# Layers two and four of an attention and two-MLP kernel, with Strassen's steps as the outer loop

## The chip, the cores and the metric

The kernel runs on one core of a Trainium2 chip. The metric is the device time of one execution in microseconds (us). TensorE (PE) does the matrix products, VectorE (DVE), ScalarE (ACT) and GpSimd (POOL) prepare operands and take results out of PSUM, and the queues of SP, ACT and POOL issue the DMAs.

## The reference

Causal attention over 2 x 12 heads (448 positions, head width 64) gives x of 896 x 768. Two MLPs follow, each with an inner width of 2048:

```python
x = attn_out.transpose(0, 2, 1, 3).reshape(896, 768)
h = x @ moe_w_in                                        # layer 1
g = np.maximum(h, 0) + alpha * np.minimum(h, 0)
x = g @ moe_w_out                                       # layer 2
h = x @ moe2_w_in                                       # layer 3
g = np.where(h >= 1, h, np.where(h <= -1, 0, (h + 1) ** 2 / 4))
out = g @ moe2_w_out                                    # layer 4
```

## The kernel before

Every operand of a product is held as a high and a low part, each in a 4-byte format that TensorE multiplies; a product of two 128-deep tiles takes three matmuls of 448 columns (high x high, high x low, low x high). A tile of the left side is `[128, 2, 448]`, for one depth tile and one batch `b` (0 or 1). Weights come from HBM as 8-byte numbers into `w_raw`, SP issues the DMA. The helper `cast` makes the upper piece `top` of each number (line L226, on POOL), `join` puts a 4-byte weight together from `w_raw` and `top` on DVE (L235), ACT makes the high part of `w_split` (L272 for layers 1 and 3, L547 for layers 2 and 4) and DVE subtracts to get the low part (L276, L552). `w_split` has three buffers.

Layers 1 and 3 (`run_layer`, products at L443) loop over 16 tiles `f` of the inner width, 36 matmuls each. `activate` (L360 to L370) and `split_g` (L347, L348) make the left tiles of the next layer from the results, and `sum_ops` (L397 to L409) makes sums S1 to S4 of them.

Layers 2 and 4 (`class Strassen`, products at L647) treat the product as a 2 x 2 block product. Its blocks are the two batches, the left and right half of the 768 output columns, and two parts of the depth. `NPAIR = 6` pairs of depth tiles, 12 of the 16, go through Strassen's scheme: seven products in place of eight, with weight quarters B11, B12, B21, B22, their sums T1 to T4 (`weight_sum`, L527, L530, L533, L536), and left sides A11, A12, A22 and S1 to S4. The last four depth tiles (`FREE`) are multiplied plainly, as items `n0` and `n2`. The loop outside is `m`, the three groups of 128 output columns in each half; inside it run the nine `ITEMS`. So every left side is gone through once for each `m`.

S2, S3 and S4 are written to DRAM by `keep`, and read back by `load_left` (L619) into places that are named by hand (`place`, the tags `g..`), then split again by ACT (`left_high`, L623) and DVE (`left_low`, L627). As there are not places for all, three tiles of each of A12, A22 and S4 (`SHIFTED`) are read again from DRAM for every further `m` (`AGAIN`, `RELOAD`; names beginning with `sA` in the trace). `copies` (L685, ACT) takes partial results out of PSUM, and `total` (L691 in layer 2, L699 in layer 4) adds the rest. In layer 2 the results of `m` 0 and 1 also go to DRAM and come back (`load_kept`, L589).

The program is written in the order in which each engine executes it: no scheduler moves anything. Each engine works through its own queue in order, and a wait at its head holds up all behind it.

Of the kernel before, what the change touches and what calls it, by code (L numbers as in the profile page):

```python
# [8 lines left out]
F32 = mybir.dt.float32  # L9
# [13 lines left out]
def attention_moe_moe_kernel(ctx: ExitStack, tc: tile.TileContext, qk, v, w1, w2, w3, w4, alpha, out):  # L23
# [8 lines left out]
    nc = tc.nc  # L32
# [86 lines left out]
    class Weights:  # L119


        def __init__(self):
            self.chunks, self.full, self.home = [], [], []
            for layer in (1, 3):
                w_in = {1: w1, 3: w3}[layer]
                for f in ORDER[layer][2 * (layer > 1):]:
                    self.add_full(w_in[f])
                self.add(layer, 0, "n0")
                for m in range(MH):
                    for i in range(len(ITEMS)):  # L130
# [973 lines left out]
```

## Time and profile before

| | us |
|---|---|
| median of 3 runs | 531.25 (529.7 to 532.61) |
| the profiled execution | 531.14 |
| its span, first to last instruction | 529.4 |
| PE busy | 520.2, 2947 matmuls |
| DVE busy | 394.1 |
| ACT busy | 293.0 |
| POOL busy | 256.3 |

Between the profiled execution's own time and its span lie 1.7 us that the trace does not show. Busy time of PE counts matmuls from their start to a modelled end, and they overlap; where PE loses time is seen from the distance between the starts of its matmuls.

### The profile page before, as it was taken

The numbers are of one execution on the slowest core, as the hardware profiler recorded it, in microseconds if no ns is written. First come the engines' busy times: TensorE is split into PE (matmuls) and PEld (weight loads), VectorE is DVE, ScalarE is ACT, GpSimd is POOL, SyncE is SP. The second block draws the span as 40 slices with busy tenths as digits, with TensorE's granted clock in tenths as the row PEclk, the third lists the DMA queues.
The fourth block names the chain that finished last, engine by engine and source line by source line (L and its number), as shares of the span: only waits on it lengthen the run. The fifth ranks groups of instructions, "written<-read, shape, count | busy, mean of one in ns | idle before, by whom it ended". The sixth has DMA issues, their size and how long they took to land.

```text
span 529.4 us, 8617 instructions
## 1 busy us (share of the span) xinstructions
PE 520.2 (98%) x2947; PEld 456.0 (86%) x2947; DVE 394.1 (74%) x650; ACT 293.0 (55%) x607; POOL 256.3 (48%) x346
## 2 busy tenths in 40 slices
PE   8999999999999999999999999999999999999995
PEld 4566679999999999899999989999999998999994
DVE  5798866677777958976685968777878489767842
ACT  6899976455555564624333665565565646243340
POOL 7677745655546661353334226555556513534210
PEclk9899999999999999999999999999999999999999
DMA  6556315356468283575675545554673735756521
GB/s 190 173 151 202 97 50 190 112 191 203 173 204 261 90 249 112 190 254 180 198 268 175 195 151 176 188 195 131 226 251 109 235 113 174 262 194 194 206 69 52
DMA packets 38971, 93.08 MB, mean 176 GB/s; under 512 B 5824, under 2 KB 24384, under 8 KB 38928
## 3 DMA queue, kind: packets, MB, share of 16 engines
q1 hardware_dynamic: 32640, 72.06, 41.8%
q0 software_dynamic: 5568, 19.96, 11.1%
q10 hardware_dynamic: 720, 0.52, 0.3%
q8 instruction: 23, 0.38, 0.3%
q14 instruction: 20, 0.16, 0.1%
HBM read 76.92 MB, written 15.60 MB: 175 GB/s over the span
## 4 chain that ended last, share of the span: by engine, by line
PE 87%; DVE 5%; ACT 4%; issue 1%; POOL 1%; DVEq 0%; ACTq 0%; POOLq 0%
PE ps L443 43%; PE ps L647 32%; PE ps L916 4%; PE ps L837 4%; PE ps L899 3%; PE ps L830 2%; ACT w_split L547 2%; DVE w_split L552 1%; DVE s L627 1%; DVE wf L235 1%; PE ps L99 1%; ACT s L623 1%; POOL pexp L874 1%; ACT act_g L364 0%; DVE wf L533 0%
## 5 line engine op out<-in xcount | busy, mean ns | idle before, releaser
L443 PE MATMUL ps<-x,w_split 128*128 128x448 f32 x1152 | 234.6, 366 | 0.0
L443 PEld LDWEIGHTS ps<-x,w_split 128*128 128x128 f32 x1152 | 216.1, 188 | 17.8 <-DVE x L610 0.6
L647 PE MATMUL ps<-g,w_split 128*128 128x448 f32 x648 | 135.8, 366 | 0.0
L647 PEld LDWEIGHTS ps<-g,w_split 128*128 128x128 f32 x648 | 121.7, 188 | 10.6
L226 POOL CAST top<-w_raw 128x768 f16<-128x768 bf16 (+1 forms) x59 | 72.4, 1233 | 78.1 <-DMA w_raw<-w 73.6
L547 ACT CAST w_split<-wf 128x768 fp32r<-128x768 f32 (+1 forms) x56 | 44.2, 789 | 84.0 <-PE ps L647 29.6
L647 PE MATMUL ps<-s,w_split 128*128 128x448 f32 x324 | 69.4, 367 | 1.2 <-ACT u L685 1.2
L647 PEld LDWEIGHTS ps<-s,w_split 128*128 128x128 f32 x324 | 60.7, 188 | 7.2 <-ACT u L685 1.9
L552 DVE TENSOR_TENSOR w_split<-wf,w_split 128x768 fp32r<-128x768 f32 (+1 forms) x56 | 53.6, 957 | 14.2 <-ACT w_split L547 13.7
L348 POOL TENSOR_TENSOR g<-act_g,g 128x448 fp32r<-128x448 f32 x36 | 45.5, 1269 | 36.9 <-ACT g L347 36.9
L874 POOL TENSOR_SCALAR pexp<-pexp,stat 128x384 f32<-128x384 f32 (+3 forms) x79 | 38.8, 511 | 16.7 <-DVE stat L866 8.4
L857 ACT ACTIVATE pexp<-pexp,stat 128x128 f32<-128x128 f32 (+3 forms) x84 | 43.7, 524 | 5.1 <-DVE stat L848 4.8
L370 DVE SCALAR_TENSOR_TENSOR act_g<-ps,act_g 128x448 f32<-128x448 f32 x36 | 22.2, 620 | 29.3 <-ACT act_g L360 14.4
L235 DVE SCALAR_TENSOR_TENSOR wf<-w_raw,top 128x768 uint32<-128x768 uint32 (+1 forms) x32 | 31.1, 972 | 16.7 <-POOL top L226 16.7
L848 DVE CUSTOM_DVE_ANT_0 pexp<-ps,mask 128x128 f32<-128x128 f32 (+3 forms) x84 | 33.0, 452 | 5.9 <-POOL ident masks.py:199 3.5
L627 DVE TENSOR_TENSOR s<-s 128x448 fp32r<-128x448 f32 x48 | 31.0, 689 | 7.6 <-ACT s L623 7.5
L235 DVE SCALAR_TENSOR_TENSOR ps<-w_raw,top 128x768 uint32<-128x768 uint32 x27 | 35.8, 1327 | 0.3
L619 POOL DMA_DIRECT2D s<-d x36 | 19.4, 543 | 30.7 <-PE ps L647 29.8
L272 ACT CAST w_split<-ps 128x768 fp32r<-128x768 f32 x27 | 21.4, 793 | 20.0 <-DVE ps L235 19.9
L348 POOL TENSOR_TENSOR g<-wf,g 128x448 fp32r<-128x448 f32 x12 | 13.9, 1156 | 35.0 <-ACT g L347 35.0
L370 DVE SCALAR_TENSOR_TENSOR wf<-ps,wf 128x448 f32<-128x448 f32 x24 | 14.9, 620 | 18.2 <-ACT wf L360 9.7
L347 ACT CAST g<-act_g 128x448 fp32r<-128x448 f32 x36 | 20.2, 567 | 12.0 <-DVE act_g L370 11.2
(89 smaller groups left out, 615.1 us busy)
## 6 DMA issues: line engine op xcount, KB each, us to landing
w_raw<-w SPq DMA_DIRECT2D x29, 767.8 KB, 4.4
w_raw<-w SPq DMA_DIRECT2D x30, 511.8 KB, 4.3
s<-d POOLq DMA_DIRECT2D x36, 224.0 KB, 4.0
d<-wf SPq DMA_DIRECT2D x24, 224.0 KB, 1.9
sA<-dA POOLq DMA_DIRECT2D x24, 224.0 KB, 4.5
w_raw<-w SPq DMA_DIRECT2D x21, 255.8 KB, 3.9
qk<-qk SPq DMA_DIRECT2D x10, 448.0 KB, 3.8
dA<-act_g SPq DMA_DIRECT2D x12, 224.0 KB, 2.3
```

The lines of the kernel that those rows point to most:

```text
L226: (side.copy if side is nc.scalar else side.tensor_copy)(d[:, c], src[:, c])
L235: nc.vector.scalar_tensor_tensor(out=w[:, a:b], in0=t.rearrange("p (n two) -> p n two", two=2)[:, c, 0], scalar=13, in1=top[:, c], op0=ALU ...
L348: nc.gpsimd.tensor_sub(t[:, 1, :], g, f32(t[:, 0, :]))
L370: nc.vector.scalar_tensor_tensor(out=d, in0=ps[:, :S], scalar=floor, in1=g, op0=ALU.max, op1=last)
L443: nc.tensor.matmul(ps[b][:, :S], lhsT=ws[:, part, k * 128:(k + 1) * 128], rhs=src[b, kk][:, xp], start=first and part == 0 and xp == 0, st ...
L547: nc.scalar.copy(s[:, 0, :n], w)
L552: nc.vector.tensor_sub(s[:, 1, :n], w, f32(s[:, 0, :n]))
L627: nc.vector.tensor_sub(t[:, 1, :], f32(t[:, 1, :]), f32(t[:, 0, :]))
L647: nc.tensor.matmul(ps[:, :S], lhsT=ws[:, part, k * 128:(k + 1) * 128], rhs=g_t[src[0], src[1] + k][:, xp], start=first and k == ks[0] and ...
L848: nc.vector.tensor_tensor_reduce(out=self.pexp[p][:, o:o + w], in0=b[:, :w], in1=mask3 if i == 3 else mask[:, 384 - w:], scale=-SCALE, sca ...
L857: nc.scalar.activation(out=e, in_=e, func=AF.Exp, bias=self.st[p][:, 0, n:n + 1], scale=-1.0, accum_out=self.st[p][:, 1, n:n + 1],)
L874: nc.gpsimd.tensor_scalar(out=e, in0=e, scalar1=self.st[p][:, 2, n:n + 1], scalar2=1.0, op0=ALU.mult, op1=ALU.mult)
```

## The change

`NPAIR` becomes 8: all sixteen depth tiles go through Strassen's scheme, and `n0`, `n2` and their weights are gone. The loops change places: the seven `STEPS` are outside, and inside each the three column groups, in four units: group 0 with depth tiles 0 to 5, the last two depth tiles for all three groups, group 1 and group 2 with tiles 0 to 5. A unit uses one `w_split` tile (six 128 x 128 blocks) and 18 matmuls; a layer has `NU = 28` units, numbered 0 to 27 below. All left tiles and the weight quarters take their places in SBUF from one list, first in, first out (`Places`). A left side is used up within its step, so nothing is read twice from DRAM, and in layer 2 no result goes to DRAM. The tables `LOAD`, `LOW`, `OUT_LOW` and `DONE` say in which unit a tile is loaded, split, and a result made. In layers 2 and 4 the cast of a weight chunk is shared by POOL and ACT (`half_tops`: half each for the first chunks of a layer, later a third on POOL), `w_raw` has three buffers instead of two, and `top` is made one chunk earlier. The last result of a layer, C21, is not added to anything but is read straight from PSUM. The first tile of layer 3 takes all depth tiles of batch 0 first.

The core of the diff:

```diff
-    NPAIR = 6
-    PAIRS = [f for k in range(NPAIR) for f in (k, NPAIR + k)]
-    FREE = list(range(2 * NPAIR, NF))
-    ORDER = {1: FREE[:1] + PAIRS + FREE[1:], 3: PAIRS + FREE}
-    FIRST = {13: "B11", 14: "B21", 15: "B12"}
-    DEPTH = dict(B11=range(NPAIR), B21=range(NPAIR, 2 * NPAIR), n0=FREE)
-    DEPTH.update(n2=DEPTH["n0"], B12=DEPTH["B11"], B22=DEPTH["B21"])
-    RIGHT = "B12", "B22", "n2"
-    ITEMS = "B11", "n0", "B21", "T1", "T2", "T4", "T3", "n2", "B22"
-    AHEAD = {6: ("B11",), 7: ("n0",), 8: ("B21",)}
-    NOW = {0: ("B22",), 4: ("n2",)}, {0: ("B12",), 1: ("B22",), 4: ("n2",)}
-    NEXT = {6: (0,), 7: (1,)}
-    SHIFTED = 0, 1, 2
+    NPAIR = NF // 2
+    WHOLE = 6
+    ORDER = [f for k in range(NPAIR) for f in (k, NPAIR + k)]
+    STEPS = ("B11", "A11", "B"), ("B21", "A12", "A"), ("T1", "S1", "D"), ("T2", "S2", "B"), \
+        ("B22", "S4", "D"), ("T3", "S3", "B"), ("T4", "A22", "B")
+    PARTS = 0, None, 1, 2
+    NU = len(STEPS) * len(PARTS)
+    QUARTERS = "B11", "B21", "B12", "B22"
+    class Places:
+
+
+        def __init__(self):
+            self.free = [("g", b, f) for f in range(NF) for b in range(NB)]
+            self.at = {}
+
+        def take(self, name, k):
+            kind, i, j = self.at[name, k] = self.free.pop(0)
+            pool = gpool if kind == "g" else xpool
+            return pool.tile([128, 2, S], F32R, tag=f"{kind}{i}_{j}", name=f"{name}_{k}", bufs=1)
+
+        def put(self, name, k):
+            self.free.append(self.at.pop((name, k)))
...
-            t = wp.tile([128, 2 * KD * 128], U32, tag="w_raw", name="w_raw")
+            t = wp.tile([128, 2 * KD * 128], U32, tag="w_raw", name="w_raw", bufs=3)
...
+        def half_tops(self):
+            i = self.n_top
+            if i < len(self.chunks):
+                self.n_top += 1
+                t, first, end = self.raw[i][0]
+                self.top[i] = top = self.free_tops.pop(0)
+                self.raw[i] = [(t, first, end, top[:, :end])]
+                for j, side in enumerate((nc.gpsimd, nc.scalar)):
+                    src = t.bitcast(BF16).rearrange("p (n four) -> p n four", four=4)[:, :, 2]
+                    d = top.bitcast(F16).rearrange("p (n two) -> p n two", two=2)[:, :, 1]
+                    a = end // 2 if i % 32 < 22 else end // 3
+                    c = slice(a, end) if j else slice(0, a)
+                    (side.copy if j else side.tensor_copy)(d[:, c], src[:, c])
...
-            if self.n_top <= self.n_split:
+            if self.n_top <= self.n_split + 1:
...
+                if layer == 3 and i == 0:
+                    for b in range(NB):
+                        ks = [(k + MH * b) % KD for k in range(KD)]
+                        for k in ks:
+                            products({b: t[:, b]}, ws, x_t, k, k, k == ks[0], k == ks[-1])
...
-        AGAIN = {1: "A12", 4: "A22", 7: 4}
-        RELOAD = {2: ("A22",), 5: (4,)}
+        LOW = {"S2": (2, 2, 3, 3, 4, 4, 5, 6), "S4": (14, 14, 14, 15, 15, 15, 16, 16),
+               "S3": (17, 17, 17, 17, 18, 19, 20, 20)}
+        LOAD = {"S2": (0, 0, 1, 1, 2, 2, 3, 4), "S4": (12, 12, 12, 12, 13, 13, 13, 13),
+                "S3": (15, 15, 15, 16, 16, 16, 17, 17)}
+        OUT_LOW = {"C11": 14, "C12": 21, "C22": 24, "C21": 27}
+        DONE = {"u1": 2, "C11": 6, "u5": 10, "u2": 16, "C12": 18, "C22": 22, "C21": 26}
...
+        def make(self, j):
...
+            step, m = j // len(PARTS), PARTS[j % len(PARTS)]
+            name, f = STEPS[step][0], self.f
+            at = {"T1": "B11", "T2": "B11", "T3": "B12", "T4": "B11"}.get(name, name)
+            w = f[at, m]
+            if name != at:
+                a = {"T1": "B12", "T2": "B22", "T3": "B22", "T4": "B21"}[name]
+                nc.vector.tensor_sub(w, f[a, m], w)
+                if name in ("T3", "T4"):
+                    places.put(a, m)
+            s = wp.tile([128, 2, KD * 128], F32R, tag="w_split", name="w_split", bufs=3)
+            self.ws[j] = s
+            nc.scalar.copy(s[:, 0], w)
             yield
+            self.join(j + 1)
             yield
+            nc.vector.tensor_sub(s[:, 1], w, f32(s[:, 0]))
+            if name in ("T3", "T4"):
+                places.put(at, m)
+
+        def join(self, j):
+            step, m = j // len(PARTS), PARTS[j % len(PARTS)]
+            if step < len(QUARTERS):
+                q = QUARTERS[step]
+                t = places.take(q, m).rearrange("p a b -> p (a b)")[:, :KD * 128]
+                if wts.n_top <= wts.n_split + 1:
+                    wts.half_tops()
+                wts.join_next(t.bitcast(U32))
+                self.f[q, m] = f32(t)
+                wts.run(wts.load())
...
+            first = step < 3
+            ws = self.ws.pop(j)
+            banks = self.bank.setdefault(bank, [])
+            if first and m in (0, None):
+                if m == 0:
+                    banks.clear()
+                    banks.append(single(ps_3) if bank == "B" else pair()[:, 0])
+                else:
+                    if bank == "B":
+                        self.shared = pair()
+                    banks += [single(ps_o) if bank == "B" else pair()[:, 0], self.shared[:, int(bank != "B")]]
+            whole, rest = range(WHOLE), range(WHOLE, NPAIR)
+            if m is None:
+                for m in range(MH):
+                    self.mult(banks[m], ws, m * len(rest), name, rest, first and m > 0, m == 0)
             else:
+                self.mult(banks[m], ws, 0, name, whole, first and m == 0, m > 0)
+            ks = rest if j % len(PARTS) == 1 else whole if j % len(PARTS) == MH else ()
+            for k in ks:
+                places.put(name, k)
...
+        def load_left(self, j):
+            for name, units in self.LOAD.items():
+                for k in range(NPAIR):
+                    if units[k] == j:
+                        nc.gpsimd.dma_start(out=f32(left_tile(name, k)[:, 1, :]), in_=sums[name, k])
...
+                g, k = self.output(name, m)
+                for c, copy, queue in ((slice(0, 256), nc.vector.tensor_copy, nc.sync), (slice(256, S), nc.scalar.copy, nc.scalar)) \
+                        if end else ((slice(0, S), None, nc.gpsimd if name == "C11" else nc.sync),):
+                    if copy:
+                        copy(t[:, c], b[:, c])
+                    queue.dma_start(out=out[k * 128:(k + 1) * 128, g * S + c.start:g * S + c.stop], in_=t[:, c])
...
+            for j in range(NU):
+                self.products(j)
+                make = self.make(j + 2)
+                if j == 0:
+                    wts.run(make)
+                if j < 4:
+                    n = (4, 1, 2, 1)[j]
+                    interleave(late[:n], [])
+                    late = late[n:]
+                self.load_left(j)
+                next(make, None)
+                self.totals(j)
+                work = [make, self.left_low(j), self.x_low(j)]
+                while work:
+                    for w in list(work):
+                        if next(w, self) is self:
+                            work.remove(w)
+                self.left_high(j + 1)
+                self.x_high(j + 1)
+            self.totals(NU)
```

PE, the start of layer 2. Before, a row of three matmuls has the next depth tile each time: B11 with A11 (`g0_0` to `g0_5`), then the plain item `n0`, which reads `g0_12` to `g0_15` and `g1_12` to `g1_15`.

```order
L647 MATMUL ps1_2409<-g0_4_2060,w_split_2322 128x448 x3
L647 MATMUL ps1_2409<-g0_5_2199,w_split_2322 128x448 x3
L647 MATMUL ps_2407<-g0_12_1471,w_split_2390 128x448 x3
L647 MATMUL ps_2407<-g0_13_2331,w_split_2390 128x448 x3
L647 MATMUL ps_2407<-g0_14_2397,w_split_2390 128x448 x3
L647 MATMUL ps_2408<-g1_12_1476,w_split_2390 128x448 x3
L647 MATMUL ps_2408<-g1_13_2336,w_split_2390 128x448 x3
L647 MATMUL ps_2408<-g1_14_2401,w_split_2390 128x448 x3
L647 MATMUL ps_2407<-g0_15_2437,w_split_2390 128x448 x3
L647 MATMUL ps_2408<-g1_15_2439,w_split_2390 128x448 x3
```

After, at the same place, the second unit (weights `w_split_2374`) is the last two depth tiles of A11 for the three column groups, and the third (`w_split_2417`) goes back to depth tile 0 for group 1.

```order
L530 MATMUL ps1_2398<-A11_4_1986,w_split_2302 128x448 x3
L530 MATMUL ps1_2398<-A11_5_2116,w_split_2302 128x448 x3
L530 MATMUL ps1_2398<-A11_6_2248,w_split_2374 128x448 x3
L530 MATMUL ps1_2398<-A11_7_2388,w_split_2374 128x448 x3
L530 MATMUL ps1_2444<-A11_6_2248,w_split_2374 128x448 x3
L530 MATMUL ps1_2444<-A11_7_2388,w_split_2374 128x448 x3
L530 MATMUL ps_2443<-A11_6_2248,w_split_2374 128x448 x3
L530 MATMUL ps_2443<-A11_7_2388,w_split_2374 128x448 x3
L530 MATMUL ps1_2444<-A11_0_1473,w_split_2417 128x448 x3
L530 MATMUL ps1_2444<-A11_1_1599,w_split_2417 128x448 x3
L530 MATMUL ps1_2444<-A11_2_1728,w_split_2417 128x448 x3
```

What moved: a left side stays in use for four units, where before each item took another left side.

ACT, the start of layer 2. Before: the splits of the last results (`g0_15`, `g1_15`), then the high parts of S2 (`s2_0` to `s2_5`) between the high parts of the weights (`w_split` from `wf`).

```order
L377 CAST g0_15_2437<-ps_2351 128x448
L377 CAST g1_15_2439<-ps_2351 128x448
L547 CAST w_split_2455<-wf_2346 128x768
L623 CAST s2_0_2443<-s2_0_2443 128x448
L623 CAST s2_1_2445<-s2_1_2445 128x448
L623 CAST s2_2_2447<-s2_2_2447 128x448
L547 CAST w_split_2504<-wf_2274 128x768
L685 COPY u1_2510<-ps1_2409 128x448
L623 CAST s2_3_2449<-s2_3_2449 128x448
L623 CAST s2_4_2451<-s2_4_2451 128x448
```

After: `S2_0` to `S2_3` stand two by two ahead of the high part of a weight chunk, and ACT also has its share of the cast (`top` from `w_raw`).

```order
L316 CAST S1_7_2464<-s1_2397 128x448
L496 CAST w_split_2471<-B11_2_2419 128x768
L187 CAST top1_71<-w_raw_2380 128x384
L574 CAST S2_0_2439<-S2_0_2439 128x448
L574 CAST S2_1_2441<-S2_1_2441 128x448
L496 CAST w_split_2511<-B21_0_2473 128x768
L610 COPY u1_2513<-ps1_2398 128x448
L187 CAST top0_70<-w_raw_2423 128x512
L574 CAST S2_2_2467<-S2_2_2467 128x448
L574 CAST S2_3_2469<-S2_3_2469 128x448
L496 CAST w_split_2550<-B21_None_2515 128x768
L610 COPY u1_2552<-ps1_2444 128x448
```

What moved: the tiles of S2 stand two by two over several units now, where six stood in two items before; the high part of B21's first chunk (`w_split_2511`) stands right behind `S2_1`, and the casts are new on ACT.

POOL, the same place. Before: whole casts (`top` from `w_raw`) between loads of S3 and S4 (S2 was loaded by SP).

```order
L226 CAST top1_71<-w_raw_2262 128x768
L619 DMA s3_0_2492<-d3_0_1604 128x448
L619 DMA s3_1_2494<-d3_1_1737 128x448
L619 DMA s3_2_2496<-d3_2_1870 128x448
L619 DMA s4_0_2498<-d4_0_1666 128x448
L619 DMA s4_1_2500<-d4_1_1799 128x448
L619 DMA s4_2_2502<-d4_2_1932 128x448
L619 DMA s3_3_2533<-d3_3_1999 128x448
L619 DMA s3_4_2535<-d3_4_2138 128x448
L619 DMA s3_5_2537<-d3_5_2278 128x448
L226 CAST top0_70<-w_raw_2344 128x512
```

After: the low parts of the last tiles of A12 and A22 and of S1, the loads of S2, and POOL's share of the casts.

```order
L317 TENSOR_TENSOR A12_7_2432<-g_2395,A12_7_2432 128x448
L317 TENSOR_TENSOR A22_7_2436<-g_2396,A22_7_2436 128x448
L567 DMA S2_0_2439<-dS2_0_1546 128x448
L567 DMA S2_1_2441<-dS2_1_1675 128x448
L317 TENSOR_TENSOR S1_7_2464<-s1_2397,S1_7_2464 128x448
L567 DMA S2_2_2467<-dS2_2_1804 128x448
L567 DMA S2_3_2469<-dS2_3_1933 128x448
L187 CAST top1_71<-w_raw_2380 128x384
L567 DMA S2_4_2507<-dS2_4_2062 128x448
L567 DMA S2_5_2509<-dS2_5_2194 128x448
L187 CAST top0_70<-w_raw_2423 128x256
L567 DMA S2_6_2548<-dS2_6_2332 128x448
```

What moved: the loads of S2 are on POOL, behind the low parts of `A12_7`, `A22_7` and `S1_7`; those of S4 and S3 come from unit 12 on.

## Rows read from the trace of the kernel before

**Rows 1.** The page's first part: busy us (share of the span) xinstructions of each engine.

```profile
PE 520.2 (98%) x2947; PEld 456.0 (86%) x2947; DVE 394.1 (74%) x650; ACT 293.0 (55%) x607; POOL 256.3 (48%) x346
```

**Rows 2.** Busy time by stretch: layer 1, then layer 2 (us, busy of each engine).

```profile
78.16:191.30 113.14, 113.14 (x560) 104.88 (x560) 82.63 (x91) 63.61 (x107) 65.36 (x52) 1.00 0.55 184
191.30:299.73 108.43, 107.84 (x524) 98.07 (x523) 83.93 (x112) 50.14 (x89) 41.55 (x63) 1.00 0.62 208
```

**Rows 3.** Line L647, PE: duration ns min/median/max, first and last start us.

```profile
L647 PE MATMUL ps<-g,w_split x648: 360/365/369, 191.3 to 519.5; 128*128 128x448 f32 x162
...
L647 PE MATMUL ps<-s,w_split x324: 358/368/475, 207.1 to 523.2; 128*128 128x448 f32 x162
...
L647 PE MATMUL ps<-sA,w_split x72: 362/368/369, 236.3 to 509.2; 128*128 128x448 f32 x72
```

**Rows 4.** PE in order of time, layer 2: start us, us, what, xcount [idle before].

```profile
207.09 3.81 PE L647 MATMUL ps<-s,w_split 128*128 128x448 f32 x18
210.74 3.81 PE L647 MATMUL ps<-g,w_split 128*128 128x448 f32 x18
215.14 3.99 PE L647 MATMUL ps<-s,w_split 128*128 128x448 f32 x18 [0.59 <-ACT u L685]
...
251.21 3.88 PE L647 MATMUL ps<-s,w_split 128*128 128x448 f32 x18
254.93 5.12 PE L647 MATMUL ps<-g,w_split 128*128 128x448 f32 x24
```

**Rows 5.** PE in order of time, from layer 2 into layer 3.

```profile
299.57 30.60 PE L443 MATMUL ps<-x,w_split 128*128 128x448 f32 x148
```

**Rows 6.** PE in order of time, layer 4.

```profile
436.20 3.81 PE L647 MATMUL ps<-g,w_split 128*128 128x448 f32 x18
440.60 3.90 PE L647 MATMUL ps<-s,w_split 128*128 128x448 f32 x18 [0.59 <-ACT u L685]
```

**Rows 7.** The chain that ended last, its piece before 215.14: start us, us, what.

```profile
210.41 0.96 DVE wf L533
...
211.47 0.84 ACT w_split L547
```

**Rows 8.** Groups of instructions in layer 2: xcount | busy us, mean ns | idle before.

```profile
L552 DVE TENSOR_TENSOR w_split<-wf,w_split 128x768 fp32r<-128x768 f32 x21 | 21.2, 1011 | 4.0 <-ACT w_split L547 3.8
L547 ACT CAST w_split<-wf 128x768 fp32r<-128x768 f32 x22 | 18.4, 836 | 30.1 <-PE ps L647 11.6 <-DVE wf L536 8.6 <-DVE wf L530 6.9
L627 DVE TENSOR_TENSOR s<-s 128x448 fp32r<-128x448 f32 x24 | 15.6, 693 | 2.5 <-ACT s L623 2.4
L226 POOL CAST top<-w_raw 128x768 f16<-128x768 bf16 x12 | 13.6, 1139 | 22.3 <-DMA w_raw<-w 17.8 <-DVE s L627 4.5
L623 ACT CAST s<-s 128x448 fp32r<-128x448 f32 x24 | 12.0, 567 | 0.0
L235 DVE SCALAR_TENSOR_TENSOR wf<-w_raw,top 128x768 uint32<-128x768 uint32 x11 | 11.7, 1063 | 10.4 <-POOL top L226 10.4
...
L691 DVE TENSOR_TENSOR u<-ps,u 128x448 f32<-128x448 f32 x10 | 6.2, 616 | 1.6 <-PE ps L647 1.6
...
L527 DVE TENSOR_TENSOR wf<-wf 128x768 f32<-128x768 f32 x3 | 2.9, 952 | 0.0
```

**Rows 9.** Groups of instructions in layer 1, same columns.

```profile
L348 POOL TENSOR_TENSOR g<-act_g,g 128x448 fp32r<-128x448 f32 x18 | 23.1, 1288 | 17.4 <-ACT g L347 17.4
...
L401 DVE TENSOR_TENSOR wf<-wf 128x448 f32<-128x448 f32 x6 | 8.3, 1383 | 0.2
```

**Rows 10.** Line L619 in layer 2: the issues on POOL, and the way to landing.

```profile
L619 POOL DMA_DIRECT2D s<-d x18: 536/536/752, 191.5 to 285.8; - x18
...
DMA to landing us min/median/max: 2.7/3.9/6.7
```

**Rows 11.** All engines in order of time, the end of the program.

```profile
523.58 0.69 DVE L699 TENSOR_TENSOR u<-ps,u 128x320 f32<-128x320 f32 x2 [3.02 <-PE ps L647]
524.14 0.34 SPq L700 DMA_DIRECT2D out<-u  x1
```

More of the change, by code (lines that the diff above doesn't have):

```diff
@@ L464, in run_layer @@
         deferred = []
[L465 removed]
+        for i, f in enumerate(ORDER):
             if layer == 1 and f in early:
@@ L471, in run_layer @@
                 ps = {b: t[:, b] for b in range(NB)}
-                ks = [k + h for k in range(MH) for h in (0, MH)] if layer == 3 and i == 0 else range(KD)
-                for n, k in enumerate(ks):
-                    products(ps, ws, x_t, k, k, n == 0, n == KD - 1)
             if wts.n_used > 1:
-                if i + 2 < NF:
-                    wts.run(wts.tops_of())
-                ops = later.ahead(i)
-                interleave(*((late, ops) if i + 1 == NF else (ops, late)))
+                wts.fill()
@@ L498, in __init__ @@
+        OUT_LOW = {"C11": 14, "C12": 21, "C22": 24, "C21": 27}
+        DONE = {"u1": 2, "C11": 6, "u5": 10, "u2": 16, "C12": 18, "C22": 22, "C21": 26}
         def __init__(self, layer):
             self.layer = layer
-            self.f, self.ws, self.bank, self.u, self.kept, self.left, self.loaded = {}, {}, {}, {}, {}, {}, {}
-        def convert(self, m, name):
-            wts.fill()
-            self.f[m, name] = wts.split_quarter()
-            yield
-            wts.run(wts.load())
-        def split(self, m, name, steps=2):
-            if name not in ("T1", "T3"):
-                self.weight_sum(m, name)
-            self.high(m, name)
-            for _ in range(steps):
-                yield
-            self.low(m, name)
@@ new lines, in join @@
+        def join(self, j):
[7 more added lines that the diff above has]
+                self.f[q, m] = f32(t)
+                wts.run(wts.load())
+        def ahead(self, i):
+            if i < NF - 2:
+                join, high, low = wts.split_ops()
+                return [join, high, lambda: wts.run(wts.load()), low]
+            if i == NF - 2:
+                self.join(0)
+            gen = self.make(i + 2 - NF)
+            return [lambda: next(gen, None)] * 3
@@ L644, in mult @@
+        def mult(self, ps, ws, at, name, ks, first, last):
             for k in ks:
@@ new lines, in load_left, with left_high @@
+        def load_left(self, j):
[3 more added lines that the diff above has]
+                        nc.gpsimd.dma_start(out=f32(left_tile(name, k)[:, 1, :]), in_=sums[name, k])
+        def left_high(self, j):
+            for name, units in self.LOW.items():
+                for k in range(NPAIR):
+                    if units[k] == j:
+                        t = left[name, k]
+                        nc.scalar.copy(t[:, 0, :], f32(t[:, 1, :]))
@@ new lines, in left_low, with outputs, output @@
+        def left_low(self, j):
+            for name, units in self.LOW.items():
+                for k in range(NPAIR):
+                    if units[k] == j:
+                        t = left[name, k]
+                        nc.vector.tensor_sub(t[:, 1, :], f32(t[:, 1, :]), f32(t[:, 0, :]))
+                        yield
+        def outputs(self, j, at):
+            return [(name, j - u) for name, u in at.items() if u <= j < u + MH]
+        @staticmethod
+        def output(name, m):
+            return int(name[1] == "2"), m + MH * (name[2] == "2")
@@ new lines, in x_high, with x_low @@
+        def x_high(self, j):
+            if self.layer == 2:
+                for name, m in self.outputs(j, self.OUT_LOW):
+                    b, k = self.output(name, m)
+                    t = x_t[b, k] = places.take(f"x{b}", k)
+                    nc.scalar.copy(t[:, 0, :], self.u[name, m])
+        def x_low(self, j):
+            if self.layer == 2:
+                for name, m in self.outputs(j, self.OUT_LOW):
+                    t = x_t[self.output(name, m)]
+                    nc.vector.tensor_sub(t[:, 1, :], self.u.pop((name, m)), f32(t[:, 0, :]))
+                    yield
```

392 lines of the change are left out of this document (83 added, 309 removed).

## The prediction

> **What bounds the kernel now.** I first read the page's busy times: PE is busy 98% of the span, DVE 74% [rows 1]. As matmuls overlap, a busy PE need not be a PE at its pace, so I went to the distance between starts. In layer 2, 18 matmuls take from 207.09 to 210.74, that is 3.65 us or 0.2028 us each; the next 18 take from 210.74 to 215.14, 4.40 us, with an idle mark before the last row; later the same number takes from 251.21 to 254.93, 3.72 us or 0.2067 each [rows 4]. So PE has two paces, 0.2028 and 0.2067, both without an idle mark, and one real hole. Layer 4 has the same hole, 436.20 to 440.60 [rows 6]. The chain shows what fills it: DVE sums of weights and ACT's high parts follow one upon the other [rows 7]. By stretch, DVE is busy 82.63 of 113.14 us in layer 1 and 83.93 of 108.43 in layer 2 [rows 2]. The kernel is thus bound by PE's number of matmuls almost everywhere, and for one moment in each of layers 2 and 4 by the chain DVE and ACT.
>
> **What goes.** The trace has 648 + 324 + 72 = 1044 matmuls at L647 [rows 3]. After, each layer has 28 units of 18, 504, both 1008: 36 fewer. At 0.2028 that is **7.30 us**. Layers 1 and 3 and attention keep theirs, in the same order on every engine until layer 1's results.
>
> The holes: 4.40 less 3.65 is 0.75 in each layer [rows 4, 6], **1.50** together. They come where T2 times S2, T4 and T3 must be ready within some 24 us of the layer's start. After, T1's first unit is number 8 and T2's number 12, and the sums are made one to a unit; I let both holes go.
>
> The slow pace: from 215.14 to 299.57 [rows 4, 5] stand 408 matmuls (522, less the 78 of the four items before 207.09 and twice 18). At 0.2028 they would take 82.74 us, not 84.43: **1.69**. The pace changed at the hole of layer 2, but did not at that of layer 4: 0.75 is all that is lost there. I don't know what chooses it. With no hole I let PE go on at 0.2028, since layer 1 ends and layer 4 runs so; the bound on the other side is a rival below.
>
> Layer 3's first 148 matmuls start within 30.23 us (30.60 less the last one's 0.37 [rows 3, 5]); 147 steps of 0.2028 make 29.81: **0.42** lost while the x tiles come in. After, batch 0 is multiplied first, and the last x tile is needed 33 matmuls or 6.7 us after unit 27, for one ACT and one DVE instruction. I let it go.
>
> The Trainium skill, "TensorE: Matmul & The Clock Gate", § Back-to-back issue gap, gives the warm distance of two matmuls as columns over 2.4 GHz plus 2.5 ns. For 448 columns that is an estimate of 189 ns, by which the 36 would give 6.8 us. The trace has 203 and 207 ns, so the measurement decides.
>
> **What is added or moved.** DVE in a layer like 2, by mean durations [rows 8]: four more weight sums at 0.952 (16 for 12), three more chunk-sized low parts at 1.011 (28 x 768 columns for 21 x 768 and 6 x 512), 12 fewer left lows at 0.693 (24 for 36), three fewer adds at 0.616, and the four sums of layer 1's last pair, which now fall here, at 0.62 to 1.38 each [rows 8, 9]; I take 1.0. Sum: 3.8 + 3.0 - 8.3 - 1.8 + 4.0 = 0.7. About 84.6 of the 102.2 us that 504 matmuls take: DVE holds on average. Layer 1 gets one more pair of sums, 4 us on 82.63: hidden under 113 us.
>
> ACT gets 16 shares of casts a layer. No row has this cast on ACT; POOL takes 1.139 for a whole one, ACT 0.836 for a high part of the same size [rows 8], so half or two thirds lies between 0.4 and 0.8. At 0.6 it is 9.6, with three more high parts at 0.836, less 12 left highs at 0.567 and three copies at 0.5: about 54 of 102 us, where it had 50.14 [rows 2]. POOL loses work.
>
> The places cost nothing as far as the list, followed by hand, goes: every take gets a place whose last reader stands in an earlier unit. The nearest are `S3_3` to `S3_5`, loaded in unit 16 into places of `S2_0` to `S2_2`, which unit 15 reads first, so they are free 0.6 to 1.8 us into unit 15. With 3.9 us to landing [rows 10] they are there early in unit 16, and are split from its end on; the cover is those 2 us, and without it ACT's next weight part would wait.
>
> The tight place is the start. In units 0 to 9 DVE has 10 joins (1.063), 10 lows (1.011), 4 weight sums (0.952), 8 S2 lows (0.693), 5 adds and totals (0.616) and those 4 sums: 10.6 + 10.1 + 3.8 + 5.5 + 3.1 + 4.0 = 37.1 us (35.6 to 38.7), against 36.5 for ten units of 3.65. The low of unit j + 2 is made in unit j, so there is about a unit of lead for that lag. The chain through S2: after layer 1's last matmul come four ACT instructions of 0.567, a total and a high, 3.5 us; POOL makes two low parts at 1.288 [rows 9], then issues `S2_0` and `S2_1` at 0.536 [rows 10]: 7.1. Landing 3.9: 11.0. Behind them on ACT waits the high part of `B21_0`, and behind that on DVE its low part: 0.57 + 0.84 + 1.01, 13.4. Unit 4 needs it at 14.6. With the longest landing, 6.7 [rows 10], it is 1.6 late.
>
> So the new loss is between 0 and some 2.2 us a layer (1.6 by landing, up to 0.6 where DVE's lag adds to it). As most landings are near 3.9, I take 0.5 a layer, **1.0**.
>
> The tail: two adds of 0.69 together after the last matmul, then the DMA [rows 11]. After, a DVE and an ACT copy run side by side; 0 to 0.3 less, counted as nothing, and nothing hides it.
>
> **Sum.** The profiled execution took 531.14, 1.7 of it outside its span of 529.4, and stands 0.11 under the median of 531.25. 531.14 - 7.30 - 1.50 - 1.69 - 0.42 + 1.0 = 521.2, by the median **521.3**.
>
> **Rivals.**
> *A new hole at the start.* Landings near 6.7, or DVE lagging more than its lead: 1.5 to 4 us in each layer, 523 to 528. For it speaks that DVE's ten units hold more than PE's; against it that POOL, whose work makes DVE's two-input instructions longer where both run (L401 takes 1.383, L527 with more columns 0.952 [rows 8, 9]), has less to do.
> *The slow pace everywhere.* If PE falls into 0.2067 at layer 2 and stays, 1584 matmuls lose 0.0039 each, 6.2 us: 527.5. In one layer alone, 2.0: 523.3. One of the two holes of before changed the pace, the other not.
> *Slower.* POOL must issue S2's loads while DVE works without a break, and all of the weight chain on ACT stands behind them. If an issue takes p in place of 0.536, `S2_5` is issued 8.0 + 6p after the start, and unit 6 (due at 21.9) is ready at 14.3 + 6p. At p above 2.4 both layers lose 6.8 us each, more than the whole gain. At 3.1 it is 11 a layer, 542. Against it: 18 such issues took 536 to 752 ns [rows 10] with DVE busy 77% of layer 2 [rows 2].
> For this mechanism the Trainium skill, "SBUF — State Buffer", § A bandwidth-pool intuition that's wrong, has a rule: a DMA issued by POOL takes about 620 ns alone and about 3100 beside a DVE copy, as POOL can't write its descriptors. The issues in this trace do not show it.
> *No gain.* The start loses 4 to 6 us in each layer: 528.6 to 533.8. A DMA that takes twice its time could do it; the trace has none over 6.7.
>
> **How the numbers follow.** A change of 0.5% (2.7 us) is about what a measurement can tell from none. Chances: forecast (519 to 523.5) 0.60, hole at the start 0.17, slow pace 0.10, no gain 0.05, slower 0.08 (0.04 for POOL's issues, the rest for what I don't see). Faster 0.87, same 0.05, slower 0.08. The range, 519.0 to 527.5, takes in no new loss (520.3) with 1.3 for the spread of runs, and the first two rivals.
>
> **What would show it.** 1008 matmuls in layers 2 and 4; the first start in layer 2 to the first in layer 3 is 102.2 us plus new holes. PE's row of 18 stays at 3.65. Units 4 to 10 are where a hole stands if there is one, with ACT or DVE as releaser, and ACT's wait for S2 ahead of it. Units 16 to 20 show S3's loads. Wrong would be: rows of 18 at 3.72 or more, POOL issues over 1 us, or idle marks of PE in layers 1 and 3, where DVE has more sums.

## The result, and the profile after

The changed kernel takes 523.53 us (median of four runs, 522.38 to 526.02); before, beside it, 530.56 (529.70 to 532.61). The ratio is 0.9868 [0.982, 0.9917]: 7.0 us faster, where 10.0 had been forecast; the time is inside the predicted range and 2.2 us above the predicted 521.3. Its profiled execution took 524.10 with a span of 522.2 us.

The first part of its page answers to [rows 1]:

```profile
PE 513.9 (98%) x2911; PEld 447.9 (86%) x2911; DVE 410.1 (79%) x632; ACT 302.1 (58%) x609; POOL 236.5 (45%) x304
```

PE has 36 matmuls fewer; DVE has more to do and ACT a little more. The sums by stretch, layer 1 to layer 4 in order (us; busy of each engine with its number of instructions; granted clock, DMA share, GB/s), answer to [rows 2]:

```profile
76.25:189.57 113.32, 113.32 (x563) 104.83 (x559) 91.75 (x91) 63.91 (x106) 61.14 (x46) 1.00 0.47 157
189.57:295.45 105.88, 104.71 (x506) 94.29 (x505) 88.53 (x112) 56.27 (x93) 34.52 (x44) 1.00 0.52 180
295.45:414.49 119.04, 119.04 (x578) 108.11 (x577) 90.42 (x91) 64.71 (x107) 58.98 (x44) 1.00 0.44 148
414.49:518.73 104.24, 103.12 (x505) 94.30 (x503) 78.23 (x96) 49.56 (x81) 30.31 (x43) 1.00 0.50 166
```

PE in order of time, layer 2 and the start of layer 4 (start us, us, what, xcount [idle before]), to be held against [rows 4] and [rows 6]:

```profile
189.57 14.75 PE L530 MATMUL ps<-A,w_split 128*128 128x448 f32 x72
204.60 0.67 PE L530 MATMUL ps<-A,w_split 128*128 128x448 f32 x2 [0.28 <-ACT w_split L496]
205.65 6.11 PE L530 MATMUL ps<-A,w_split 128*128 128x448 f32 x28 [0.39 <-DVE w_split L500]
212.26 8.94 PE L530 MATMUL ps<-A,w_split 128*128 128x448 f32 x42 [0.51 <-ACT u L610]
221.05 59.68 PE L530 MATMUL ps<-S,w_split 128*128 128x448 f32 x288
280.57 15.04 PE L530 MATMUL ps<-A,w_split 128*128 128x448 f32 x72
...
414.49 15.04 PE L530 MATMUL ps<-A,w_split 128*128 128x448 f32 x72
430.31 0.67 PE L530 MATMUL ps<-A,w_split 128*128 128x448 f32 x2 [0.79 <-ACT w_split L496]
431.31 14.46 PE L530 MATMUL ps<-A,w_split 128*128 128x448 f32 x70 [0.32 <-DVE w_split L500]
445.60 58.53 PE L530 MATMUL ps<-S,w_split 128*128 128x448 f32 x288
```

Two things are to be seen. Layer 2 is whole for units 0 to 3 (72 matmuls) and has holes in units 4 and 5 (the one of 0.51 us before 212.26 is at the 13th matmul of unit 5; the expectations of E1 and E4 below call that unit 6); layer 4 has them in unit 4 alone. And the pace: 288 matmuls take 221.05 to 280.57, 0.2067 us each, in layer 2, but 445.60 to 503.96, 0.2026, in layer 4. Layer 3 has no hole at all and is still 119.04 us long, which is 576 times 0.2067.

With the first start of each layer as bound, the two profiled spans compare like this. A hole here is a distance of two starts over 0.23 us, and its cost is what exceeds 0.2028. The third column is the changed kernel profiled once more (E6 below), the others are experiments.

| us | before | after | after again (E6) | S2 later (E1) | before, outputs on SP (E5) |
|---|---|---|---|---|---|
| ahead of layer 1 | 78.09 | 76.25 | 76.22 | 75.87 | 76.44 |
| layer 1 | 113.19 | 113.31 | 113.65 | 113.37 | 113.19 |
| layer 2 (holes) | 108.29 (0.86) | 105.88 (2.08) | 103.83 (1.41) | 102.14 (0) | 106.64 (0.85) |
| layer 3 (holes) | 117.18 (0.32) | 119.04 (0) | 117.91 (0.89) | 118.00 (0.99) | 117.03 (0.27) |
| layer 4 (holes) | 106.79 (0.85) | 104.23 (1.65) | 105.26 (2.96) | 102.31 (0) | 108.43 (0.85) |
| slow matmuls in layers 2, 3, 4 | 407, 28, 0 | 417, 576, 71 | 72, 69, 0 | 0, 70, 0 | 0, 6, 405 |
| from the last matmul's end | 5.82 | 3.48 | 3.47 | 3.48 | 3.49 |
| span | 529.36 | 522.20 | 520.34 | 515.18 | 525.22 |

Of the 7.16 us between the two spans, layers 2 and 4 give 4.97, the end 2.34 and the head 1.84; layers 1 and 3 take 1.98 back.

Where the holes come from stands in three engines at layer 2's start, 189.57. First ACT, then POOL, then DVE, in order of time:

```profile
194.65 1.10 ACT L316 CAST A<-g 128x448 fp32r<-128x448 f32 x2 [0.61 <-DVE g L333]
...
202.68 1.14 ACT L574 CAST S<-S 128x448 fp32r<-128x448 f32 x2 [4.99 <-DMA S<-dS]
203.72 0.83 ACT L496 CAST w_split<-B 128x768 fp32r<-128x768 f32 x1
```

```profile
195.29 3.37 POOL L317 TENSOR_TENSOR A<-g,A 128x448 fp32r<-128x448 f32 x2 [1.96 <-ACT A L316]
198.60 1.29 POOL L567 DMA_DIRECT2D S<-dS  x2
```

```profile
190.93 1.91 DVE L210 SCALAR_TENSOR_TENSOR B<-w_raw,top 128x768 uint32<-128x768 uint32 x1
192.76 1.32 DVE L500 TENSOR_TENSOR w_split<-B,w_split 128x768 fp32r<-128x768 f32 x1
194.00 1.14 DVE L333 SCALAR_TENSOR_TENSOR g<-ps,g 128x448 f32<-128x448 f32 x2
...
197.56 1.91 DVE L500 TENSOR_TENSOR w_split<-B,w_split 128x768 fp32r<-128x768 f32 x1
```

DVE makes a join and a low part before it adds layer 1's last totals at 194.00, so ACT's high parts of `A12_7` and `A22_7` end 6.2 us after the layer's start, and POOL's two low parts take 3.37 us. The loads of `S2_0` and `S2_1` leave at 198.60, 9.0 us after the start. ACT then stands idle for 4.99 us before the split of S2, and the high part of `B21_0` waits in its queue until 203.72. Unit 4 is due at 204.17. The line of the loads, over the start of layer 2:

```profile
L567 POOL DMA_DIRECT2D S<-dS x8: 538/538/740, 198.6 to 208.3; - x8
...
  ACT S L574: 6.4, 4
...
DMA to landing us min/median/max: 3.9/5.7/7.0
```

The issue itself takes what it took in [rows 10]; the landing has a median of 5.7 us in place of 3.9, and ACT waited 6.4 us for it in four places. The two loads that unit 4 waits for are the quickest, `S2_0` and `S2_1` with 4.05 and 3.88 us; the slow ones come later. `S2_5` took 7.0 us, and behind its split stands ACT's copy that frees the PSUM bank for the hole in unit 5. In layer 4 `S2_1` itself took 5.7.

### The profile page after: what moved, and what is told of

The parts are those of the page before. It is cut to its first block, busy times and chain, and to the rows that moved or that the text cites. A ratio compares the mean times of both kernels' runs of the same rounds, so it can differ in the third digit from the quotient of the medians.

```text
span 522.2 us, 8426 instructions
## 1 busy us (share of the span) xinstructions
PE 513.9 (98%) x2911; PEld 447.9 (86%) x2911; DVE 410.1 (79%) x632; ACT 302.1 (58%) x609; POOL 236.5 (45%) x304
## 5 line engine op out<-in xcount | busy, mean ns | idle before, releaser
L530 PE MATMUL ps<-S,w_split 128*128 128x448 f32 x576 | 118.2, 367 | 0.0
L530 PEld LDWEIGHTS ps<-S,w_split 128*128 128x128 f32 x576 | 108.1, 188 | 9.8
L317 POOL TENSOR_TENSOR A<-g,A 128x448 fp32r<-128x448 f32 x48 | 60.5, 1263 | 112.7 <-ACT A L316 112.7
L530 PE MATMUL ps<-A,w_split 128*128 128x448 f32 x432 | 90.4, 368 | 2.3 <-ACT w_split L496 1.1
L530 PEld LDWEIGHTS ps<-A,w_split 128*128 128x128 f32 x432 | 80.6, 188 | 11.4 <-ACT w_split L496 1.8
L333 DVE SCALAR_TENSOR_TENSOR g<-ps,g 128x448 f32<-128x448 f32 x64 | 39.3, 619 | 43.8 <-ACT g L328 25.5
L496 ACT CAST w_split<-B 128x768 fp32r<-128x768 f32 x42 | 35.1, 836 | 60.8 <-PE ps L530 34.2
L201 POOL CAST top<-w_raw 128x768 f16<-128x768 bf16 x34 | 49.2, 1446 | 43.9 <-issue 35.1
L500 DVE TENSOR_TENSOR w_split<-B,w_split 128x768 fp32r<-128x768 f32 x42 | 44.2, 1053 | 20.9 <-ACT w_split L496 20.4
L210 DVE SCALAR_TENSOR_TENSOR B<-w_raw,top 128x768 uint32<-128x768 uint32 x24 | 30.6, 1275 | 0.4 <-POOL top L187 0.4
```

The lines of the kernel that those rows point to most:

```text
L201: (side.copy if side is nc.scalar else side.tensor_copy)(d[:, c], src[:, c])
L210: nc.vector.scalar_tensor_tensor(out=w[:, a:b], in0=t.rearrange("p (n two) -> p n two", two=2)[:, c, 0], scalar=13, in1=top[:, c], op0=ALU ...
L317: nc.gpsimd.tensor_sub(t[:, 1, :], g, f32(t[:, 0, :]))
L333: nc.vector.scalar_tensor_tensor(out=g, in0=ps[:, :S], scalar=floor, in1=g, op0=ALU.max, op1=last)
L496: nc.scalar.copy(s[:, 0], w)
L500: nc.vector.tensor_sub(s[:, 1], w, f32(s[:, 0]))
```

## The experiments

**E1: S2 loaded and split later.** The theory from these rows: ACT is stuck behind S2 with weights in its queue. The rival: DVE simply has too much to do in the first ten units.

```diff
-        LOW = {"S2": (2, 2, 3, 3, 4, 4, 5, 6), ...
+        LOW = {"S2": (4, 4, 5, 5, 9, 9, 10, 11), ...
-        LOAD = {"S2": (0, 0, 1, 1, 2, 2, 3, 4), ...
+        LOAD = {"S2": (1, 1, 2, 2, 5, 5, 6, 7), ...
```

> The changed kernel has holes of 2.08 us in layer 2 and 1.65 in layer 4, in units 4 and 6, with ACT idle 5 us for the landing of S2 just before. Here S2 is loaded one unit later and split in units 4 to 11 instead of 2 to 6. Theory one (ACT's queue stands still behind S2's landings): the holes fall to 0.5 us or less in each layer, and PE, without a hole, stays at its faster pace of 0.2028 us per matmul through layers 2 to 4 (the changed kernel had 0.2067 for 993 matmuls in layer 2 and 3): in all 5 to 8 us less, 516 to 519 us. Theory two (DVE lags, since its two-input instructions take 1.9 us beside POOL's instead of 0.95): over 1 us of holes remains in each layer, 521 to 524 us.

Measured: 518.0 us (three runs at 517.0 to 518.9, one at 524.9 without a trace), ratio to before 0.978 [0.971, 0.985], span 515.2. PE in order of time, layer 2, and the sums of layers 2 and 4:

```profile
189.25 29.35 PE L530 MATMUL ps<-A,w_split 128*128 128x448 f32 x144
218.43 58.53 PE L530 MATMUL ps<-S,w_split 128*128 128x448 f32 x288
276.80 14.76 PE L530 MATMUL ps<-A,w_split 128*128 128x448 f32 x72
```

```profile
189.24:291.39 102.15, 102.15 (x506) 94.65 (x504) 89.03 (x112) 56.19 (x93) 33.79 (x44) 1.00 0.56 187
...
409.39:511.70 102.31, 102.31 (x505) 94.46 (x503) 78.65 (x97) 49.69 (x81) 30.45 (x43) 1.00 0.51 172
```

No idle mark is left, with DVE as busy over layer 2 as in the changed kernel (89.03 us, there 88.53). That does not yet exclude the rival, since two of S2's eight low parts have left the first ten units; E4, where DVE keeps its order, weighs it. 504 matmuls at 0.2027 us are what a layer costs when nothing is late.

**E4: the same loads at the same units, by SP.**

```diff
-    nc.gpsimd.dma_start(out=f32(left_tile(name, k)[:, 1, :]), in_=sums[name, k])
+    (nc.sync if name == "S2" else nc.gpsimd).dma_start(out=..., in_=sums[name, k])
```

> S2's loads go by SP's queue instead of POOL's, in the same units. They are then not behind the low parts of A12 and A22 on POOL, and S2_0 should land some 5 us earlier. Theory one (ACT's queue behind S2's landings): the holes of units 4 and 6 fall below 0.5 us in all. Theory two (DVE's lag): the two holes of unit 4 (0.65 and 0.75 at 204 us in the changed kernel) stay, only that of unit 6 goes; 521 to 524 us.

Measured: 521.47 us, ratio 0.9846 [0.9778, 0.9914], span 522.8. SP issues the first loads at 196.07, 4.2 us after the layer's start at 191.88, as it has no low parts ahead of them. PE in layers 2 and 4:

```profile
191.88 29.83 PE L530 MATMUL ps<-A,w_split 128*128 128x448 f32 x144
221.55 59.68 PE L530 MATMUL ps<-S,w_split 128*128 128x448 f32 x288
...
414.99 29.92 PE L530 MATMUL ps<-A,w_split 128*128 128x448 f32 x144
444.75 59.68 PE L530 MATMUL ps<-S,w_split 128*128 128x448 f32 x288
```

The holes are gone (0.21 us in all, at 206.7), as the first theory said, with DVE's instructions in the order of the changed kernel. So the rival of E1, DVE's work in the first units, costs next to nothing once S2's loads are early and off POOL; E8 leaves them late and on POOL. But the profiled execution took 524.84, no less than the changed kernel's: from that one small gap on, all 1,508 matmuls to the program's end run at 0.2067, 5.9 us in layers 2 to 4. Its four timed runs go from 518.13 to 524.84.

**E8: only the splits later, the loads left as the change has them.**

```diff
-        LOW = {"S2": (2, 2, 3, 3, 4, 4, 5, 6), ...
+        LOW = {"S2": (4, 4, 5, 5, 9, 9, 10, 11), ...
```

> Only the splits of S2 on ScalarE and VectorE come later; its loads stay where the change put them on POOL. Theory one (the loss is the order on ScalarE, which waits for S2 with the high part of the next weights queued behind it): holes of at most 0.5 us in layer two and in layer four, although POOL issues the first loads of S2 at about 9 us after the layer's start as before; time 516 to 521. Theory two (the late transfers themselves, or POOL's time for issuing them, are the loss): holes of 1 us or more in each of the two layers, 521 to 525.

Measured: 520.16 us, ratio 0.9843 [0.9816, 0.987], span 516.5. The line of the loads in layer 2, which begins at 189.82:

```profile
L567 POOL DMA_DIRECT2D S<-dS x8: 538/540/740, 198.9 to 208.0; - x8
...
DMA to landing us min/median/max: 3.9/5.5/6.8
```

The loads leave as late as after the change (9.0 us) and land as slowly, yet the holes are 0.43 us in layer 2 and 0.32 in layer 4, for 2.08 and 1.65 (in the three profiles with the order of the change, the first, E2 and E6, 0.68 to 2.08 and 1.65 to 2.96). So most of the loss is the order in ACT's queue (the edit moves S2's splits on DVE too, but E4 left those where they were), and the slow transfer costs mainly what is queued behind its reader. By time alone this run can't be told from the changed kernel, whose ratio is 0.9868 [0.982, 0.9917]; the holes tell them apart.

What is left has another cause. ACT, then DVE twice:

```profile
197.99 0.83 ACT L496 CAST w_split<-B 128x768 fp32r<-128x768 f32 x1
...
203.26 0.96 DVE L210 SCALAR_TENSOR_TENSOR B_None<-w_raw,top 128x768 uint32<-128x768 uint32 x1 [0.52 <-POOL top L187]
204.13 0.95 DVE L500 TENSOR_TENSOR w_split<-B,w_split 128x768 fp32r<-128x768 f32 x1
```

ACT has the high part of `B21_0` at 198.82, but DVE begins the low part only at 204.13, 14.3 us after the layer's start, behind a join that waited for POOL's `top`. That cast stands behind four of S2's loads on POOL; in E1, with two ahead of it, the low part begins at 13.7 us and there is no hole.

**E7: E1 and E4 together.** The edits are those of E1 and E4.

> S2 both loaded and split later, and its loads given to SP. Theory one (once ScalarE is no longer held by S2, nothing of S2 is on the path, so the queue of its loads is of no account): no hole over 0.3 us in layers two and four, each 102.1 to 102.5 us at the fast pace or up to 104.2 at the slow one, and a time within 0.5% of the variant with the later tables alone, 516 to 520. Theory two (POOL's issue time is still part of it): faster than that variant by 1 us or more. Theory three (SP's loads stand behind or ahead of weights and move those): holes of 0.5 us or more in layer two, 520 to 525.

Measured: 517.83 us, ratio 0.9827 [0.9788, 0.9866], span 515.7; layers 2 and 4 take 102.14 and 102.31 us without a hole. That is E1 again, the first theory: with S2 loaded and split later, the queue of its loads is of no account. Four runs lie within 517.6 to 517.9 and two at 523.0; the size of that step fits the slow pace, but these two have no trace, so it stays open.

**E3: casts back to POOL alone,** to see what the ACT shares are worth.

```diff
-                    a = end // 2 if i % 32 < 22 else end // 3
+                    a = end
+                    if j:
+                        continue
```

> The casts of layers 2 and 4 all on POOL again, ACT has none. Theory one (the start of the layer is short of POOL and DVE time): joins wait longer and DVE's two-input instructions beside POOL's get longer, holes grow to 3 to 7 us in each layer, 526 to 534 us. Theory two (POOL is 45% busy and has room): holes stay within 0.5 us of those of the changed kernel, 522 to 525 us.

Measured: 529.56 us, ratio 1.0003 [0.9977, 1.0029], span 529.3: the whole gain gone. PE in layers 2 and 4 (line numbers two higher):

```profile
209.68 16.01 PE L532 MATMUL ps<-A,w_split 128*128 128x448 f32 x70 [2.40 <-DVE w_split L502]
...
260.10 25.47 PE L532 MATMUL ps<-S,w_split 128*128 128x448 f32 x122 [0.77 <-DVE S L583]
...
435.30 0.67 PE L532 MATMUL ps<-A,w_split 128*128 128x448 f32 x2 [0.93 <-ACT w_split L498]
436.54 14.45 PE L532 MATMUL ps<-A,w_split 128*128 128x448 f32 x70 [0.56 <-DVE w_split L502]
```

Holes of 3.7 us in layer 2 and 3.8 in layer 4, the first theory. With them came the slow pace (267 matmuls of layer 2 and all 576 of layer 3, 3.3 us), a spell at half clock (last section, 1.5 us), and, as in before, one in the head. The shared casts are what makes the new order hold.

**E2: the outputs back on POOL,** for the 2.34 us at the end.

```diff
-    ... else ((slice(0, S), None, nc.gpsimd if name == "C11" else nc.sync),):
+    ... else ((slice(0, S), None, nc.gpsimd),):
```

> From the end of the last matmul to the end of the span the kernel before takes 5.8 us, the changed one 3.5, which the prediction did not have. Here only the queue of the outputs C12, C22 and C21 of layer 4 goes back from SP to POOL, as in the kernel before (the last column group still leaves by SP and ACT). Theory one (POOL comes late to the end of the program when it has issued DMAs in the last microseconds): the tail is 5.5 to 5.9 us again and all else stays, 2 us more. Theory two (the tail is shorter as the last copy is halved between DVE and ACT): the tail stays at 3.4 to 3.7.

Measured: 524.66 us, ratio 0.9901 [0.9874, 0.9929]; the end is 3.46 us and the time that of the changed kernel. Layer 2 shows 0.68 us of holes and layer 4 1.77, with the instructions of layer 2 unchanged. My first theory fell as I had put it: POOL issues an output at 517.38, 2.8 us before the last matmul ends, as in before, and nothing is late; the end is that of theory two, which E5 tests. The trace holds why POOL is not late. In these ten traces POOL's closing DRAIN, counted from POOL's last DMA, lasts the longer the more DMAs POOL has issued in the program:

| DMAs issued by POOL | 35 (E4, E7) | 51 (after, E1, E3, E6, E8) | 59 (E2) | 76 (E5) | 87 (before) |
|---|---|---|---|---|---|
| DRAIN, us | 4.3, 4.3 | 4.9, 5.0, 5.2, 5.0, 5.0 | 5.5 | 6.8 | 7.7 |

In before it runs from 520.84 to 528.58, 2.1 us after the other engines came to the end; in E2 from 517.36 to 522.82, when SP is just there.

**E5: the kernel before, with its outputs on SP,** the direct test of that.

```diff
-    ... if end else ((slice(0, S), nc.gpsimd),):
+    ... if end else ((slice(0, S), nc.sync),):
```

> The kernel before, with the outputs of layer four given to SP instead of POOL (only the choice of the queue changes). Theory one (in the profiled run of before POOL reached the end 2.1 us after the others because its DRAIN lasted 7.7 us from its last transfer of an output): the stretch from the last matmul's end to the span's end falls from 5.8 to 3.4 to 3.7 us and the time by 2 us, to 527.5 to 530 beside the profiled 531.1. Theory two (the longer end belongs to something else in the kernel before): 5.5 to 5.9 us again and no gain. On the pace of the matmuls, a further look: theory one (each stretch between two holes of TensorE runs at 202.7 or at 206.7 ns a matmul, and which one is drawn anew at each hole) says that layer three may come out at either, 116.8 or 119.0 us without holes, whatever it was in the profiled before; theory two (the pace belongs to the place in the program) says 206.7 from the hole in layer two to the end of layer two, and 202.7 elsewhere, as in before.

Measured: 526.99 us in one run (before beside it 528.16, at the least 527.34), span 525.2, the end 3.49 us; POOL's DRAIN starts at 507.75 and is over at 514.59. One run can't show 2 us in the time, but the trace's end is 2.3 us shorter with the last adds of before, so E2's theory two falls as well: 2.3 us of the change's gain are POOL's closing DRAIN, and could be had without the change. As to the pace, it is not tied to a place in the program. PE behind the holes of layers 2 and 4:

```profile
213.49 3.91 PE L647 MATMUL ps<-s,w_split 128*128 128x448 f32 x18 [0.58 <-ACT u L685]
217.23 5.03 PE L647 MATMUL ps<-g,w_split 128*128 128x448 f32 x24
...
437.16 3.98 PE L647 MATMUL ps<-s,w_split 128*128 128x448 f32 x18 [0.59 <-ACT u L685]
440.97 5.12 PE L647 MATMUL ps<-g,w_split 128*128 128x448 f32 x24
```

The 18 of layer 2 take 3.74 us with the end of the gap in them and go on at 0.2027; those of layer 4 take 3.81 and go on at 0.2067, the reverse of before, where layer 2 went on at 0.2067 [rows 4] and layer 4 at 0.2027.

**E6: the changed kernel unaltered, once more.**

> The changed kernel once more, unaltered, for what recurs. Theory one (the holes come from the order of the instructions, the pace behind each is drawn by chance): holes of 1.7 to 2.4 us in layer two and 1.3 to 2.0 in layer four at the same matmuls, while layer three may take 116.8 or 119.0 us; the stretch ahead of layer one 76 or 78 us by whether TensorE has a spell at half clock there; time 517 to 526. Theory two (the pace belongs to the place): layer three 119.0 again and 206.7 ns from the first hole of layer two to the holes of layer four.

Measured: 522.23 us, span 520.3. PE around layer 4's hole, and the line of the loads there:

```profile
428.47 0.68 PE L530 MATMUL ps<-A,w_split 128*128 128x448 f32 x2 [2.10 <-ACT w_split L496]
429.46 14.45 PE L530 MATMUL ps<-A,w_split 128*128 128x448 f32 x70 [0.32 <-DVE w_split L500]
```

```profile
DMA to landing us min/median/max: 4.3/5.6/7.4
```

The holes stand at the same units but change in size, 1.41 and 2.96 us (both outside what I had put down, one on each side). They go with the moment at which the loads leave, counted from the layer's start: in layer 2 that is 8.7 us here and 9.0 in the first profile of the change; in layer 4 it is 9.0 here and 8.2 there, where layer 3 ran at the slow pace, and `S2_1` took 5.9 us to land here, 5.7 there. E8's loads leave at 9.0 there too, and its 0.32 us of holes are best held against these 2.96. The pace of a place is not its own: layer 3 ran at 0.2027 here but for 69 matmuls, and then showed 0.89 us of holes, with DVE's low part (L249) as releaser. All four executions with a fast layer 3 (E1, E6, E7, E8) have 0.9 to 1.25 us of them and the four with a slow one (after, E2 to E4) none: the slow pace hides that DVE is a little late there.

## Why the prediction came out right

The time fell in the range, with the gain forecast 3.0 us too large. Two of the terms were wrong, and what made up for most of it was not forecast.

**36 matmuls fewer, 7.30 us: right.** Hole-free and at one pace, layer 2 takes 102.14 us (E1); before, 106.64 less its holes of 0.85 (E5): 3.65 us a layer.

**The holes, −1.50 + 1.0: mis-sized, and the place right.** They did not shrink from 1.71 to 1.0 but grew to 3.73, with 4.37 in E6 and 2.45 in E2. Releaser, units 4 and 5 and ACT's wait for S2 are as the prediction's signs had them. The chain that led to 13.4 us failed in two terms in layer 2: the totals on DVE stand behind a join and a low part (lows begun 5.7 us after the start, not 3.5), and POOL's two lows took 3.37 and not 2.58, so that ACT had S2 at 13.1 and the high part of `B21_0` began at 14.15. The landing of 3.9 held for the two loads of this chain; it failed in layer 4 (5.7 for `S2_1`) and for the later tiles, behind which stands unit 5's hole. I had followed each engine's own sum but not DVE's order ahead of layer 1's last totals.

**The slow pace, −1.69: failed.** I let it go with the hole. In the profiled execution 417 + 576 + 71 matmuls ran slow, 4.2 us, so this term went from a gain of 1.7 to a loss of 2.5. The term had no ground in the change: in E5, the kernel before, layer 2 has no slow stretch and layer 4 has one of 405. The rival that put the slow pace in one or all layers was the nearer step; E4 is close to its full case, 5.9 of the 6.2 us that it gave.

**Layer 3's start, −0.42: right,** 0.32 by the starts; no idle mark is there.

**The tail, nothing to 0.3: mis-sized,** 2.34. I had read when the last adds and DMAs end, and not that POOL's DRAIN outlasts them.

**Not in the sum:** 1.84 us ahead of layer 1. In before, TensorE has a spell at half clock (1.2 GHz). The stretch 12 to 16 us of before, and then of after (columns as above):

```profile
12.00:16.00 4.00, 4.00 (x28) 2.16 (x30) 3.00 (x13) 3.18 (x13) 1.60 (x4) 0.64 0.46 106
```

```profile
12.00:16.00 4.00, 4.00 (x37) 2.18 (x34) 3.97 (x15) 3.45 (x14) 1.68 (x3) 1.00 0.54 169
```

The granted clock is 0.64 in the mean with 28 matmuls, against 1.00 with 37; 20 matmuls from 12.4 us on take 4.27 us in before, and the same 20 take 2.72 in both E5 and the changed kernel, which is 1.55 of the 1.84. E5, the same code there, has no such spell and 76.44, and E2 to E4 have one: it belongs to the run, not to the change.

**More sums on DVE in layers 1 and 3, hidden: right in layer 1,** 0.12 longer, though DVE's time there grew by 9.1 us and not by the 4 of one pair of sums: its 13 joins took 1.72 us each, 1.29 before. In layer 3 only while the pace is slow; else some 1 us of holes (E6).

**Units 16 to 20, S3 into S2's places: right.** PE has no mark there in any run but E3, whose second hole stands at 260.10.

**POOL's issue time: as forecast.** 538 to 740 ns for S2's loads while DVE works. The figure of about 3100 ns beside a DVE copy, in the Trainium skill's "SBUF — State Buffer", § A bandwidth-pool intuition that's wrong, is not seen in any of these traces, where no issue on POOL takes over 752 ns; but beside S2's loads DVE ran instructions with two inputs, not copies, so the copy's case is not tried.

The sum with measured terms: −7.30 + 2.02 (holes) + 2.46 (pace) − 0.32 − 2.34 − 1.84 + 0.12 (layer 1) = −7.20, and the spans differ by 7.16. The forecast came within 2.2 us because two terms that I set 6.7 us too favourably (holes 2.5, pace 4.2) met two gains of 4.2 us that I had not counted. That they met was luck: the spell at half clock and the paces differ from run to run, and the DRAIN I had not read.

## What to carry to other kernels

On an engine that works in order, ask of each instruction that waits for a transfer what stands behind it: moving the reader by two to five units (E8) took the holes of the two layers from 3.73 us to 0.75, and moving the transfer as well (E1) to none. When a stage's first step needs the last results of the stage before, follow the queue of every engine that they pass, since an engine with room in its sum may still have two microseconds of other work ahead of them. And where a prediction rests on the pace of one profiled execution, look at a second: here two profiles of one kernel differ by 2 us in layer 2, of which only 0.7 are holes.

## What the runs showed that I had not expected

**Two paces.** In ten traces the 448-column matmuls run at one of two steady distances, 0.2026 to 0.2027 or 0.2067 us, at a granted clock of 1.00 (2.4 GHz) in both. Of 49 stretches of 60 or more matmuls without a distance over 0.23 us, 38 ran at the first and 11 at the second. The pace changes behind a gap, with one exception of some 30 matmuls in E3 that began and ended without one (one step of 0.225 stands at its end); a gap of 0.1 us is enough, many gaps change nothing, and the same instructions run at either. What decides it is open. The slow pace costs 2.2 us in layer 3, and a kernel without gaps (E1, E7) kept the fast one through layers 2 and 4 in the profiled executions.

**DVE and POOL beside each other.** DVE's low part took 1.91 us at 197.56, beside POOL's low parts, and 0.95 at 214.97, with POOL standing. E1 has 1.91 again at the same place.

**Half clock in the middle.** In E3, the stretch in which TensorE stood idle, then two behind it (columns as above):

```profile
206.90:209.70 2.80, 0.40 (x3) 0.03 (x2) 2.80 (x3) 2.34 (x5) 1.97 (x3) 1.00 1.01 350
210.90:214.30 3.40, 3.40 (x11) 3.03 (x10) 3.40 (x6) 2.30 (x4) 1.07 (x2) 0.51 0.85 280
214.30:218.00 3.70, 3.70 (x19) 3.41 (x19) 2.75 (x5) 1.31 (x2) 2.94 (x1) 0.99 1.01 287
```

After a hole of 2.56 us the granted clock fell to half (1.2 GHz) for 3.4 us, in which nine matmuls stood 0.372 us apart: 1.5 us lost on top of the hole. E6's hole of 2.27 us in layer 4 was followed by no such fall (granted clock 1.00 from 428.50 on).
